# Moving two spectrum loads and a state table behind an FFT reload, and three stores to other DMA queues, in a one-core S4 convolution and MLP gradient kernel

## The chip, the core and the metric

The kernel runs on one core of one Trainium2 chip. The metric is device time in microseconds (us) of one launch. The core has TensorE (PE; its weight loads are listed as PEld), VectorE (DVE), ScalarE (ACT), GpSimd (POOL) and SyncE (SP). SP, ACT and POOL each issue DMA transfers from a queue of their own; an instruction that waits in such a queue holds up all that stand behind it.

## The reference

The forward function mixes two branches by a gate, g = sigmoid(sum of u * gate_w):

```python
dt = exp(log_dt); logdA = dt * (A_re + 1j*A_im); dB = dt * (B_re + 1j*B_im)
P = exp(logdA[:, :, None] * l)                # l = 0..2047
K = einsum("dn,dnl,dn->dl", C, P, dB).real    # 448 x 2048 convolution kernel
a = irfft(rfft(u padded) * rfft(K padded))[:L] + u * Dskip
b = relu(u @ w1 + b1)**2 @ w2 + b2            # 448 -> 1792 -> 448
out = g * a + (1 - g) * b
```

The reference returns this output and the gradients of all parameters and of u for a given grad_out: fifteen outputs. L is 2048, D is 448, N is 256; the inputs and outputs are bf16.

## The kernel before, in words

The FFT convolutions are done as two stages of matmuls with constant matrices. `Ker.fwd1` (lines 224 to 246) is the first stage: for two halves hh and four groups q it multiplies 16 row tiles by `F1`, copies the results from PSUM to a staging buffer, and stores each of the eight staging buffers (448 KB) to a DRAM scratch `gd`. The store goes through DRAM because the second stage needs the data in another layout: `Ker.load_s1` (line 250) loads a quarter of gd back on SP's queue, and it depends on all eight stores. `Ker.fwd2` (line 260) is the second stage. `Ker.inv1` (line 296) and `inv2` (lines 313 and 315) are the inverse transform, which stores to a scratch `hd` (line 300) from a ring of six staging buffers and is loaded back by `load_hs` (line 306).

There are three transforms forward: u, the scaled gradient, and K. The first two run in the first part, and their spectra are stored to `sp_d`. The part in the middle runs the MLP (`dense`), interleaved by hand with the state-space recurrences over 14 chunks of channels (`period`). Until `order` is entered (`tc.manual_schedule()`, near 215 us) the order of instructions on each engine comes from a planner with a cost model; after it, each engine runs in the order in which the program is written.

The first layer of the MLP computes 14 tiles of the hidden activations (`hidden`, lines 663 to 683) and stores each to a scratch `rT_d` (512 KB) when its second half is done. The first two stores go to GpSimd's queue, the later ones to SP's.

The tail begins when K has been built and stored to `k_d`. It loads K back into `xs` (`reload_k`), loads the first spectrum, runs the last chunk's backward pass (`back_z`, line 1162), loads two more spectra by `load_sx` (line 1431, 896 KB each on SP's queue) and the state table of the second parameter tile by `load_st` (line 1422, 512 KB on GpSimd's queue), and then runs `fwd1` on K with `K.lean` set. With `lean`, each staging buffer is stored by one transfer. The eight staging buffers are all different, so fwd1 does not wait for its stores. After it come `back_p` (lines 1173 and 1175), the eight steps of `param_grads` for the first parameter tile (line 1494 and those after it, on DVE and ACT, with outputs stored by GpSimd, line 1497), the last steps of the MLP, the four loads of gd, and the last `back_s`. The three remaining spectra are then loaded.

The loop that follows takes each quarter q of the spectrum of K: `product(w, q)` multiplies it by a loaded spectrum on DVE (lines 1568 and 1569), `fwd2` computes the next quarter, and `back1` runs `inv1` on the product. For w = 0 all four quarters are done, then hd[1] is loaded back; for w = 1 the same is done with hd[2]. The spectra are read in the order (0,0), (0,1), (0,2), (0,3), (1,0), (1,1), (1,2), (1,3). The two loaded before fwd1 are (0,3) and (1,0). The state table of the second parameter tile is read by `param_grads(1)`, between the products of w = 1. Two loops over the quarters then finish the two outputs.

Of the kernel before, what the change touches and what calls it, by code (L numbers as in the profile page):

```python
# [162 lines left out]
class Ker:  # L163
# [62 lines left out]
    def fwd1(self, rhs, gd, stage, act_first=0, between=None):  # L226
        nc = self.nc
        for hh in range(2):
            for q in range(4):
                self.act_only = 4 * hh + q < act_first  # L230
                st = stage[self.stage_i % len(stage)]
                self.stage_i += 1
                for j2 in range(2):
                    ps = self.pair()
                    for jj in range(2):
                        nc.tensor.matmul(ps[jj][:, 0:D], lhsT=self.F1[:, hh * 128:(hh + 1) * 128], rhs=rhs(q * 4 + j2 * 2 + jj), start=True, stop=True)  # L236
                    self.evac2(st[:, 2 * j2:2 * j2 + 2, :], ps)
                dst = bass.AP(tensor=gd, offset=(16 * hh + q * 4) * 128 * D, ap=[[D, 128], [128 * D, 4], [1, D]])
                if self.lean:
                    (self.q2 if q % 2 == 0 or hh == 1 else nc.sync).dma_start(dst, st)  # L240
                else:
                    for g2 in range(2):
                        half = bass.AP(tensor=gd, offset=((16 * hh + q * 4) * 128 + 64 * g2) * D, ap=[[D, 64], [128 * D, 4], [1, D]])
                        (self.q2 if g2 == 0 else nc.sync).dma_start(half, st[64 * g2:64 * g2 + 64])
                if between:
                    between(4 * hh + q)
# [73 lines left out]
def kernel(ctx, tc, A_u, A_A_re, A_A_im, A_B_re, A_B_im, A_C_re, A_C_im, A_log_dt, A_Dskip,  # L320
# [3 lines left out]
    nc = tc.nc  # L324
    V, S, G_, T_ = nc.vector, nc.scalar, nc.gpsimd, nc.tensor
# [5 lines left out]
    def dscr(name, n, dt=bf16):  # L331
        return nc.dram_tensor(name, (n,), dt, kind="Internal")
# [9 lines left out]
    rT_d = dscr("rT_d", F * L)  # L342
# [58 lines left out]
    def carve(n, dt=bf16, k=0):  # L401
        nonlocal o
        w = n * (2 if dt == fp32 else 1)
        if k:
            r = RA[:, 7168:7168 + w]
        else:
            r = RA[:, o:o + w]
            o += w
        return r.bitcast(fp32) if dt == fp32 else r
    for nm, src in (("Ar", A_A_re), ("Ai", A_A_im), ("Br", A_B_re), ("Bi", A_B_im), ("Cr", A_C_re), ("Ci", A_C_im)):  # L410
        r = carve(2 * D).rearrange("p (h d) -> p h d", h=2)
# [16 lines left out]
    SB = K.t("S25", [P, 12800])  # L428
# [216 lines left out]
    def force(i):  # L645
        if held and held[0][0] <= i:
            release()

    def rows_of(tensor, j):
        return bass.AP(tensor=tensor, offset=256 * j, ap=[[8 * HW, P], [HW, 8], [1, 256]])  # L650

    def load_w1(jp):
        b = w1b[jp % 2]
        G_.dma_start(b[:, 0:3], bass.AP(tensor=B_w1.tensor, offset=B_w1.offset + 256 * jp, ap=[[F, P], [P * F, 3], [1, 256]]))
        for h in range(2):
            G_.dma_start(b[64 * h:64 * h + 64, 3], bass.AP(tensor=B_w1.tensor, offset=B_w1.offset + 384 * F + 256 * jp, ap=[[F, 64], [1, 256]]))

    def wide(half, w, x):

        pss = [K.ps(b, [P, 512]) for b in BK["h"]]  # L660
        for k in range(2):
            for dt in range(DT - 1):
                T_.matmul(pss[k][:], lhsT=w[:, dt], rhs=x(2 * half + k)[:, dt], start=(dt == 0), stop=False, skip_group_check=True)  # L663
        for k in range(2):
            h = slice(64 * k, 64 * k + 64)
            T_.matmul(pss[k][:], lhsT=w[h, 3], rhs=x(2 * half + k)[h, 3], start=False, stop=True, tile_position=(64 * k, 0), skip_group_check=True)  # L666
        return pss

    def hidden(j, half):
        pss = wide(half, w1b[j // 2 % 2][:, :, P * (j % 2):P * (j % 2) + P], lambda lb: UT[:, :, 512 * lb:512 * lb + 512])  # L670
        if half == 0:
            rcur[j], prev = rts.pop(0)
            rts.append((rcur[j], j))
            force(prev)
        r = rcur[j]
        for k in range(2):
            lb = 2 * half + k
            S.activation(r[:, 512 * lb:512 * lb + 512], pss[k][:], ACT.Relu, bias=b1_f[:, j:j + 1])  # L678
        if half == 1:
            if hold:  # L680
                held.append((j, lambda: nc.sync.dma_start(rows_of(rT_d, j), r)))
            else:
                (G_ if j < 2 else nc.sync).dma_start(rows_of(rT_d, j), r)
            if j % 2 == 1 and j // 2 + 2 < HP:
                load_w1(j // 2 + 2)

# [36 lines left out]
    def first_layer():  # L723
# [3 lines left out]
        for half in range(2):  # L727
            hidden(0, half)
            yield
# [417 lines left out]
    def back_z(c, yt, j, banks=None):  # L1147

        nonlocal zi
        h = j // 2  # L1150
        if (c, h) not in zbs:
            zbs[c, h] = zr[zi % 2]
            zi += 1
        psF = None if banks else K.psF()
        psz = [K.ps(i, [P, 512]) for i in banks] if banks else [psF[:, t] for t in range(2)]
        for b in range(16):
            for t in range(2):
                T_.matmul(psz[t][:, 32 * b:32 * b + 32], lhsT=yt[64 * t:64 * t + NY, b, :], rhs=DKc[64 * t:64 * t + NY, c % 2, 16 * (j % 2) + b].rearrange("p s a -> p (s a)"),  # L1158
                          start=True, stop=True, tile_position=(64 * t, 0), skip_group_check=True)
        if banks:  # L1160
            for t in range(2):
                S.copy(run(zbs[c, h][:, 0:1], 16 * (j % 2) + 1024 * t, [64, NA], [32, 2], [1, 16]), run(psz[t][:, 0:1], 0, [1, NA], [NA, 2], [32, 16]))
        else:
            S.copy(run(zbs[c, h][:, 0:1], 16 * (j % 2), [1024, 2], [64, NA], [32, 2], [1, 16]), run(psF[:, 0, 0:1], 0, [512, 2], [1, NA], [NA, 2], [32, 16]))  # L1164
# [13 lines left out]
    def back_s(c, Q):  # L1178

        nonlocal sps  # L1180
        cc = c % GC
        if cc == 0:
            sps = K.ps("S", [P, GC, 2, P])
        for r in range(2):
            for t in range(2):
                if r + t > 0:
                    yield
                for a in range(NA):
                    for h in range(2):
                        T_.matmul(sps[64 * h:64 * h + 64, cc, r, :], lhsT=Q[h][r][:, 1024 * t + 64 * a:1024 * t + 64 * a + 64], rhs=(nident if r == 0 and t == 1 else ident)[:],  # L1190
                                  start=(cc == 0 and r == 0 and t == 0 and a == 0), stop=(cc == GC - 1 and r == 1 and t == 1 and a == NA - 1),
                                  tile_position=(0, 64 * h), skip_group_check=True)
        if cc == GC - 1:
            stS = K.t("st", [P, 512], fp32, bufs=2)
            S.copy(stS[:], sps[:].rearrange("p q r n -> p (q r n)"))  # L1195
            for x in range(4):
                G_.dma_start(bass.AP(tensor=s_d, offset=(x * D + 64 * (c // GC)) * 256, ap=[[512, 32], [1, 512]]), stS[32 * x:32 * x + 32])  # L1197
# [221 lines left out]
    def load_st(dt, b, q_):  # L1419
        z = DSZ[dt]  # L1420
        STs[dt] = b[:, 0:2048].bitcast(fp32).rearrange("p (h k r n) -> p k r h n", h=2, k=2, r=2)
        q_.dma_start(b[:z, 0:2048].bitcast(fp32).rearrange("p (x n) -> p x n", x=4), bass.AP(tensor=s_d, offset=dt * P * 256, ap=[[256, z], [D * 256, 4], [1, 256]]))
# [7 lines left out]
    def load_sx(w, q, k, qe=nc.sync):  # L1430
        qe.dma_start(slots[k], bass.AP(tensor=sp_d[w], offset=q * 8 * D, ap=[[16 * 2 * D, P], [1, 8 * D]]))
        return slots[k].rearrange("p (a r d) -> p a r d", a=4, r=2)
# [6 lines left out]
    sx = {(0, q): load_sx(0, q, q - 1) for q in (1, 2)}  # L1439
# [28 lines left out]
    V.tensor_tensor(out=xv[0:1, 0], in0=xv[0:1, 0], in1=dsk_bc[0:1].rearrange("o (c g e) -> o c g e", g=NG, e=16), op=ALU.add)  # L1468
    for j in range(4):
        back_z(NCH - 1, YTs[NCH - 1][j], j, NT[2 * (j % 2):2 * (j % 2) + 2])  # L1470
    for q in (3, 4):
        sx[q // 4, q % 4] = load_sx(q // 4, q % 4, q + 6)
    load_st(1, SB[:, 10752:12800], G_)
    K.pairs = 3

    Gt = Pt[:, 0:7168].rearrange("p (t d) -> p t d", d=D)
# [73 lines left out]
    s1k = [b.rearrange("p (a d) -> p a d", d=D) for b in (Yf[:, 0:3584], Yf[:, 3584:7168], SB[:, 6272:9856], SB[:, 0:3584])]  # L1550
    for q in range(4):
        K.load_s1(gd[2], q, s1k[q])
    sums = back_s(NCH - 1, [Qs.pop((NCH - 1, h)) for h in range(2)])
    sx[1, 3] = load_sx(1, 3, 4)
    sx[1, 1] = load_sx(1, 1, 2)
# [63 lines left out]
    for q in range(4):  # L1619
# [30 lines left out]
        for g in range(NG):  # L1650
            dst = bass.AP(tensor=o0.tensor, offset=o0.offset + (16 * g + 2 * q) * D, ap=[[64 * D, 32], [8 * D, 2], [1, 2 * D]])
            G_.dma_start(dst, ao[32 * g:32 * g + 32].rearrange("p (h x) d -> p h (x d)", h=2))
    close(3)
    for q in range(4):
# [9 lines left out]
        for g in range(NG):  # L1664
            dst = bass.AP(tensor=o1.tensor, offset=o1.offset + (16 * g + 2 * q) * D, ap=[[64 * D, 32], [8 * D, 2], [1, 2 * D]])
# [51 lines left out]
```

## Time and profile before

| what | value |
|---|---|
| median of three runs | 741.79 us (738.06 to 744.74) |
| time of the profiled execution | 742.86 us |
| its span, first to last instruction | 741.1 us |
| granted TensorE clock, mean | 0.912 of full |
| bytes moved by DMA | 176.73 MB, mean 238 GB/s |

Times in the profile are microseconds from the start of the span. A row of the timeline gives the start, the time covered, the engine, the source line, the operation, what it writes and reads by the program's tile names, and how many instructions are merged; in brackets stands how long the engine had been idle and what released it. Engine names that end in q are the engine's queue of DMA instructions or of semaphores. Tile names are those of the storage, so `Y<-gd` is a load of gd into a tile that lies in Y's storage, and `R<-sp` is a load of a spectrum.

### The profile page before, as it was taken

What the parts mean: (1) busy time and instruction counts of PE and PEld (TensorE: products, weight loads), DVE (VectorE), ACT (ScalarE), POOL (GpSimd) and SP (SyncE); (2) the same over time, 40 slices, a digit from 0 to 9 for tenths busy, and PEclk for the clock granted to TensorE, in tenths of its full rate; (3) what the DMA queues carried; (4) which work ended last, traced back from release to release, by engine and by line L of the source; (5) the groups of instructions that cost most, each with busy time, mean ns of one, the idle gap of its engine ahead of it and who ended that gap; (6) DMA issues with size and microseconds to landing.
All of it is one profiled execution on the core that took longest, in us unless ns stands there. A gap on an engine that the chain in (4) does not pass through costs nothing.

```text
span 741.1 us, 20444 instructions
## 1 busy us (share of the span) xinstructions
PE 626.1 (84%) x8556; PEld 338.3 (46%) x8597; DVE 563.0 (76%) x928; ACT 513.8 (69%) x877; POOL 167.9 (23%) x285
## 2 busy tenths in 40 slices
PE   5957968789899987998999996989989888787666
PEld 2411323333346553655656664655655563433211
DVE  1397587676788566889999899698898886959474
ACT  2796967588777666777788777778744536598555
POOL 2252211111134311111211201102100333311543
PEclk9986976889999999999999999999999988999757
DMA  9898576829477899999998988999997949988995
GB/s 205 184 298 275 180 271 224 299 96 349 171 246 262 241 238 220 170 250 229 212 221 217 217 133 245 249 205 269 210 230 209 275 119 364 345 292 303 315 331 167
DMA packets 205276, 176.73 MB, mean 238 GB/s; under 512 B 122814, under 2 KB 185559, under 8 KB 205055
## 3 DMA queue, kind: packets, MB, share of 16 engines
q1 hardware_dynamic: 181999, 116.78, 63.8%
q0 software_dynamic: 14272, 39.68, 17.4%
q10 hardware_dynamic: 8912, 18.96, 7.0%
q8 instruction: 67, 1.10, 0.6%
q14 instruction: 26, 0.21, 0.1%
HBM read 82.90 MB, written 64.32 MB: 199 GB/s over the span
## 4 chain that ended last, share of the span: by engine, by line
PE 46%; DVE 16%; DMA 14%; ACT 11%; issue 11%; POOL 1%; ACTq 0%; DVEq 0%; POOLq 0%; SPq 0%
PE psN L663 7%; PE psS L1190 5%; PE psN L699 5%; PE psN L919 4%; PE psX L1096 3%; DMA R<-Y 3%; DVE Y L1035 3%; DVE Y L1032 3%; DVE F L1033 2%; PE psX L699 2%; PE psN L666 2%; PE psF L1158 2%; PE psN L260 2%; DMA out_dram<-X 2%; PE psN L236 2%
## 5 line engine op out<-in xcount | busy, mean ns | idle before, releaser
L699 PEld LDWEIGHTS <-U 128*128 128x128 bf16 x448 | 40.9, 100 | 44.0 <-issue 14.1
L1164 ACT CAST P<-psF 128x1024 bf16<-128x1024 f32 x52 | 53.1, 1022 | 8.9 <-PE psF L1158 8.7
L1032 DVE TENSOR_TENSOR Y<-Y,F 128x1024 bf16<-128x1024 bf16 (+3 forms) x70 | 47.9, 685 | 2.7
L1035 DVE TENSOR_TENSOR Y<-Y,F 128x1024 bf16<-128x1024 bf16 (+3 forms) x70 | 48.1, 688 | 2.4
L663 PEld LDWEIGHTS <-S 128*128 128x128 bf16 x336 | 29.9, 100 | 43.4 <-issue 17.3
L699 PE MATMUL psN<-S,U 128*128 128x449 bf16 x224 | 48.0, 355 | 1.1 <-issue 1.1
L663 PE MATMUL psN<-S 128*128 128x512 bf16 x153 | 46.2, 414 | 1.9 <-issue 1.0
L1033 DVE TENSOR_TENSOR F<-Y,F 128x1024 bf16<-128x1024 bf16 (+3 forms) x70 | 47.3, 675 | 0.0
L699 PE MATMUL psX<-D,U 128*128 128x448 bf16 x160 | 37.2, 370 | 2.1 <-ACT D L705 2.1
L1197 POOL DMA_DIRECT2D s_d<-st x28 | 14.8, 536 | 103.5 <-ACT st L1195 103.5
L691 ACT ACTIVATE U<-psN 128x1024 bf16<-128x1024 bf16 x35 | 36.1, 1031 | 1.5 <-PE psN L690 1.5
L678 ACT ACTIVATE U<-psN,b_f 128x512 bf16<-128x512 f32 x48 | 31.1, 688 | 6.2 <-PE psN L666 4.3
L1158 PEld LDWEIGHTS <-R 41*128 41x128 bf16 x1792 | 26.8, 93 | 18.3 <-issue 15.9
L919 PEld LDWEIGHTS <-U 128*128 128x128 bf16 x252 | 24.4, 101 | 23.5 <-issue 3.8
L1158 PE MATMUL psF<-S,R 41*128 41x32 bf16 x1664 | 29.5, 174 | 5.3 <-ACT P L1164 5.3
L663 PE MATMUL psN<-K,S 128*128 128x512 bf16 x100 | 26.6, 379 | 5.3 <-issue 2.9
L919 PE MATMUL psN<-S,U 128*128 128x448 bf16 x140 | 29.9, 368 | 0.0
L296 PEld LDWEIGHTS <-cb_MI 64*128 64x128 bf16 x256 | 15.7, 99 | 30.4 <-issue 22.0
L1190 PEld LDWEIGHTS <-M 128*64 128x64 bf16 x896 | 25.8, 110 | 3.8 <-issue 2.6
L1190 PE MATMUL psS<-ident,P 128*64 128x128 bf16 x896 | 27.5, 219 | 0.0
L1190 PEld LDWEIGHTS <-P 128*64 128x64 bf16 x896 | 25.9, 110 | 0.0
L1173 DVE TENSOR_TENSOR M<-P,R 128x2048 bf16<-128x2048 bf16 x14 | 17.1, 1221 | 10.2 <-ACT P L1164 10.2
(417 smaller groups left out, 1684.0 us busy)
## 6 DMA issues: line engine op xcount, KB each, us to landing
sp<-K ACTq DMA_DIRECT2D x8, 896.0 KB, 6.8
rT_d<-U SPq DMA_DIRECT2D x10, 512.0 KB, 5.1
hd<-F SPq DMA_DIRECT2D x11, 448.0 KB, 10.4
X<-gd SPq DMA_DIRECT2D x5, 896.0 KB
U<-dhT_d SPq DMA_DIRECT2D x5, 896.0 KB
rec_d<-F ACTq DMA_DIRECT2D x2, 1920.0 KB, 9.0
hd<-st ACTq DMA_DIRECT2D x8, 448.0 KB
rec<-rec_d POOLq DMA_DIRECT2D x14, 256.0 KB, 5.6
```

What stands on the lines that cost most here:

```text
L663: T_.matmul(pss[k][:], lhsT=w[:, dt], rhs=x(2 * half + k)[:, dt], start=(dt == 0), stop=False, skip_group_check=True)
L678: S.activation(r[:, 512 * lb:512 * lb + 512], pss[k][:], ACT.Relu, bias=b1_f[:, j:j + 1])
L691: S.activation(hn[j % 2][:, 8 * th:8 * th + 8, :], ps[:], f)
L699: T_.matmul(ps[:, 0:w], lhsT=hn[j % 2][:, t, :], rhs=rhs[:, t, :], start=(t == 0), stop=(t == LT - 1))
L919: T_.matmul(ps[:, 0:D], lhsT=src[j][:, P * x:P * x + P], rhs=ws[:, j, :], start=(j == 0), stop=(j == FT - 1))
L1032: V.tensor_tensor(out=run(yb, dst, [64, X2], [d0[1], n // d0[1]], [1, d0[1]]), in0=run(yb, 0, [64, X2], *src), in1=pr, op=ALU.mult)
L1033: V.tensor_tensor(out=run(vb, 0, [n, X2], [d0[1], n // d0[1]], [1, d0[1]]), in0=run(yb, 0, [64, X2], *src), in1=pi, op=ALU.mult)
L1035: return V.tensor_tensor(out=hi, in0=hi, in1=run(vb, n, [2 * n, W2], [-n, 2], [1, n]), op=ALU.add)
L1096: T_.matmul(ps[32 * g:32 * g + 32, i], lhsT=run(xb, 2048 * (1 - t) + w, [W2, 32]), rhs=Y[:, w, t, 0:NY], start=(h == 0 and t == 0), stop=( ...
L1158: T_.matmul(psz[t][:, 32 * b:32 * b + 32], lhsT=yt[64 * t:64 * t + NY, b, :], rhs=DKc[64 * t:64 * t + NY, c % 2, 16 * (j % 2) + b].rearran ...
L1164: S.copy(run(zbs[c, h][:, 0:1], 16 * (j % 2), [1024, 2], [64, NA], [32, 2], [1, 16]), run(psF[:, 0, 0:1], 0, [512, 2], [1, NA], [NA, 2], [ ...
L1190: T_.matmul(sps[64 * h:64 * h + 64, cc, r, :], lhsT=Q[h][r][:, 1024 * t + 64 * a:1024 * t + 64 * a + 64], rhs=(nident if r == 0 and t == 1 ...
```

## The change

Four places change. In `fwd1` with `lean`, which only the tail's call uses, the stores of the second half (hh = 1) alternate between GpSimd's and SP's queue as those of the first half do; before, all four of the second half were on GpSimd's. The loads of the spectra (0,3) and (1,0) and of the state table move from ahead of that `fwd1` to behind the four loads of gd. In `hidden`, the store of the third tile (j = 2) goes to GpSimd's queue instead of SP's; this store is in the first part, not in the tail.

```diff
                 if self.lean:
-                    (self.q2 if q % 2 == 0 or hh == 1 else nc.sync).dma_start(dst, st)
+                    (self.q2 if q % 2 == 0 else nc.sync).dma_start(dst, st)
...
             else:
-                (G_ if j < 2 else nc.sync).dma_start(rows_of(rT_d, j), r)
+                (G_ if j < 3 else nc.sync).dma_start(rows_of(rT_d, j), r)
...
         back_z(NCH - 1, YTs[NCH - 1][j], j, NT[2 * (j % 2):2 * (j % 2) + 2])
-    for q in (3, 4):
-        sx[q // 4, q % 4] = load_sx(q // 4, q % 4, q + 6)
-    load_st(1, SB[:, 10752:12800], G_)
     K.pairs = 3
...
     for q in range(4):
         K.load_s1(gd[2], q, s1k[q])
+    for q in (3, 4):
+        sx[q // 4, q % 4] = load_sx(q // 4, q % 4, q + 6)
+    load_st(1, SB[:, 10752:12800], G_)
     sums = back_s(NCH - 1, [Qs.pop((NCH - 1, h)) for h in range(2)])
     sx[1, 3] = load_sx(1, 3, 4)
```

`self.q2` is GpSimd's queue here (`K.q2 = G_`), `G_` is GpSimd, `nc.sync` is SP.

## The prediction, as put on record

> **What bounds the kernel now.** I read the page first, then the chain of waits from 600 us on, then the tail by stretches and by engine. The page's chain of what ended last says that no engine sets the whole time, PE the most with 46%:
>
> ```profile
> span 741.1 us, 20444 instructions
> PE 46%; DVE 16%; DMA 14%; ACT 11%; issue 11%; POOL 1%; ACTq 0%; DVEq 0%; POOLq 0%; SPq 0%
> ```
>
> The tail edits act between 608 and 690 us. The queue of SyncE and GpSimd's instructions show who sends what there:
>
> ```profile
> 610.39 2.50 SPq L1431 DMA_DIRECT2D R<-sp  x2
> 613.02 0.77 POOL L1422 DMA_DIRECT2D S<-s_d  x1 [4.22 <-PE psN L236]
> 618.81 3.39 SPq L240 DMA_DIRECT2D gd<-X  x2
> 625.87 1.50 POOL L240 DMA_DIRECT2D gd<-Y  x2 [0.31 <-ACT Y L220]
> 626.62 5.89 DMA gd<-Y
> 637.54 0.57 PE L260 MATMUL psN<-Y,P 128*64 128x448 bf16 x4 [4.34 <-DMA Y<-gd]
> ```
>
> The two spectra (R<-sp) and the state table (S<-s_d) leave before the first FFT stage of K writes gd. Of its eight stores, the last is issued at 626.62, lands 5.89 us later, at 632.5, and only then may SP load gd back (Y<-gd); PE has stood for 4.34 us when it gets the first quarter. That looks like the bound, but VectorE says otherwise:
>
> ```profile
> 625.83 1.22 DVE L1173 TENSOR_TENSOR M<-P,R 128x2048 bf16<-128x2048 bf16 x1
> 637.64 0.08 DVE L1528 DVE_READ_ACCUMULATOR Y<-Y,dtc,R 128x1 f32 x1
> 638.15 0.62 DVE L211 CAST Y<-psN 128x448 bf16<-128x448 f32 x1 [0.43 <-PE psN L260]
> ```
>
> From 625.83 to 637.72 it runs without a gap (back_p, then all of param_grads(0)). The evacuation of fwd2's first result stands behind that in its queue and waited for PE only 0.43 us. The late reload therefore costs the path 0.43 us, not 4.34.
>
> The transfers by stretch (columns after the span: busy time of PE, PEld, DVE, ACT, POOL; granted clock, DMA share, GB/s):
>
> ```profile
> 618.00:632.00 14.00, 13.45 (x62) 6.34 (x61) 13.19 (x18) 8.52 (x17) 5.45 (x8) 0.88 0.99 335
> 636.00:652.00 16.00, 14.06 (x208) 8.89 (x209) 12.34 (x13) 10.71 (x21) 6.72 (x13) 0.89 1.01 407
> 652.00:660.00 8.00, 7.11 (x58) 3.25 (x59) 4.05 (x2) 8.00 (x18) 0.97 (x2) 1.00 1.06 324
> 660.00:664.00 4.00, 3.08 (x28) 1.44 (x25) 3.25 (x2) 4.00 (x9) 0.00 (x0) 1.00 0.43 141
> 664.00:670.00 6.00, 5.14 (x38) 2.72 (x39) 5.95 (x4) 3.50 (x7) 0.00 (x0) 0.72 0.90 265
> 670.00:674.00 4.00, 2.69 (x27) 1.35 (x24) 3.93 (x5) 4.00 (x10) 1.14 (x2) 1.00 0.41 139
> ```
>
> The DMA engines are full to 632 and from 636 to 660, then half idle to 674. A second place is bound by transfers:
>
> ```profile
> 670.39 0.38 SPq L300 DMA_DIRECT2D hd<-F  x1
> 673.25 0.34 SPq L306 DMA_DIRECT2D M<-hd  x1
> 676.20 6.24 SPq L300 DMA_DIRECT2D hd<-F  x3
> 688.54 0.53 ACT L210 CAST F<-psN 128x448 bf16<-128x448 f32 x1 [5.38 <-DMA hd<-F]
> ```
>
> SP stores the last piece of hd[1] at 670.39 and may load hd back at 673.25; the stores from 676.20 stand behind those loads, and ScalarE waits 5.38 us for one of them before it can reuse its buffer. So the end follows from when hd[1] has landed, 673.25.
>
> **The change, part by part.** (1) Stores 6 and 8 of the first stage go from GpSimd's queue to SP's.
>
> ```profile
> L240 POOL DMA_DIRECT2D gd<-Y x4: 754/754/754, 623.3 to 626.6; - x4
> L240 SPq DMA_DIRECT2D gd<-X x2: 365/368/370, 618.8 to 621.8; - x2
> gd<-X SPq DMA_DIRECT2D x2, 448.0 KB
> R<-sp SPq DMA_DIRECT2D x4, 896.0 KB
> S<-s_d POOLq DMA_DIRECT2D x1, 512.0 KB, 8.7
> ```
>
> The issue falls from 0.75 to 0.37 us. (2) Two R<-sp and one S<-s_d, 2 x 896 + 512 = 2304 KB or 2.36 MB, no longer stand ahead of the stores. Six stores are left after 622.20 (618.81 + 3.39, where SP's second one is issued): 6 x 448 KB = 2.75 MB, at 335 GB/s 8.2 us, so their data is through at 630.4, and with a tail of 0.6 us (my estimate; the share of the DMA engines ends at about 632, the last store at 626.62 + 5.89 = 632.5) landed at 631.0. The gain is 1.5 us. Its bounds: 0, if the stores and not what was ahead of them fill the engines; and 3.1, if the last, issued at 626.62 as now, lands as quickly as the fastest hd store of the same size did (2.8 us, the least in the line below), at 629.4. I take 1.5, the rate of the row over the same stores.
>
> ```profile
> DMA to landing us min/median/max: 2.8/10.4/13.1
> ```
>
> Of these 1.5 us the path gets 0.43, because VectorE is not free before 637.72. **Term A: -0.43 us**, if the reload is at least that much earlier; 0 if it isn't. If it lets ScalarE and PE run ahead as well, at most the whole 1.5.
>
> (3) The moved loads now run behind the reload. Who needs them:
>
> ```profile
> 660.72 2.02 DVE L1568 TENSOR_TENSOR X<-R,S 128x3584 bf16<-128x3584 bf16 x1 [2.65 <-ACT S L211]
> 670.26 0.72 ACT L1498 ACTIVATE D<-S,dtc 128x512 f32<-128x512 bf16 x1
> ```
>
> The first spectrum is read at 660.72 (the second one product later), the table at 670.26. Behind the reload (4 x 896 KB = 3.67 MB) the first is through after 4.59 MB, at 407 GB/s 11.3 us after about 634.5, near 646, the second near 648: 14 us ahead of need. GpSimd issues the table after its param_grads stores, near 637, which puts load_raw(1) back 0.77 us; it feeds the same step at 670.26. Cost of both nothing, as long as products and inv1 cover them. SP issues them in some 0.4 us each, with nothing due in its queue before the first hd store, near 649.
>
> (4) What is late next is the hd[1] stores, which share SP's ring with the moved loads. From 636 to 670 the rows above move 6.51 + 2.59 + 0.56 + 1.59 = 11.25 MB; with 2.36 more it is 13.6, of which seven hd stores are 3.2 MB. Pure store traffic and pure loads run at
>
> ```profile
> DMA packets 1608, 1.42 MB, mean 355 GB/s; under 512 B 49, under 2 KB 1605, under 8 KB 1607
> ```
>
> (687 to 691, SP's queue alone) and 407 GB/s: 3.2 / 0.355 + 10.4 / 0.407 = 9.0 + 25.6 = 34.6 us. Started 1.5 us earlier, at 634.5, the ring is empty at 669.1, 0.9 us before the last hd store is issued (670.39 - 0.43 = 669.96). **Term B: 0.** Without the head start and with the stores at the mixed 324 GB/s it is empty at 671.5, and the last store lands 1.5 us late; nothing absorbed would be 2.36 MB at 407 GB/s, 5.8 us late. I take 0, since the idle stretches 660 to 664 and 670 to 674 are seen.
>
> At this row a rule of the skill speaks against the change: the Trainium skill, DMA: Bandwidth & Descriptors, section Queues, rings and completion order, says that each DMA engine takes the descriptors of one queue in ring order. The trace agrees, in the 5.38 us that ScalarE waits for a store behind loads. By the rule alone, with no idle time counted, the sum would be +5.4 us.
>
> (5) rT_d's third store (j = 2) goes from SP to GpSimd.
>
> ```profile
> 66.50 16.96 SPq L250 DMA_DIRECT2D X<-gd  x2
> 92.70 0.56 SPq L683 DMA_DIRECT2D rT_d<-U  x1
> 97.33 0.32 SPq L250 DMA_DIRECT2D X<-gd  x1
> 98.10 0.72 POOL L713 DMA_DIRECT2D DBT_d<-S  x1 [11.21 <-ACT S L712]
> L683 POOL DMA_DIRECT2D rT_d<-U x2: 907/930/952, 75.5 to 80.8; - x2
> ```
>
> SP holds it from 83.46 to 92.70, but what follows waits for its buffer until 97.33, so nothing is won. On GpSimd its 0.93 us lie inside an idle time of 11.21. **Term C: 0.** Uncovered it would cost those 0.93 us.
>
> **The sum**: 742.86 us for the profiled execution (741.1 span, 1.8 around it) - 0.43 + 0 + 0 = 742.4. The median of the three runs is 741.79, 1.07 lower, so there **741.4 us**; its own range is 740.3 (all 1.5 us pass) to 742.9 (term A empty, 1.1 lost in term B).
>
> **The rivals.** *Backlog* (slower): the moved loads hold SP's ring beyond 669.96, the last hd[1] store lands late, the load of hd starts after 673.25 and ScalarE's wait at 688.54 moves with it. It decides once the ring empties after 669.96. Price 1.5 - 0.43 = 1.1 to 5.8 - 0.43 = 5.4 us; middle 3.2, so 745.0. For it: no idle time from 636 to 660. Against it: the two half-empty stretches.
>
> *PE stays fast* (faster). Where the first stage starts, PE stands and then runs slowly:
>
> ```profile
> 615.68 0.91 PE L236 MATMUL psN<-F,cb_F1BD 128*128 128x448 bf16 x2 [2.20 <-issue]
> 616.00:622.00 6.00, 6.00 (x19) 2.56 (x18) 4.03 (x6) 3.72 (x7) 1.51 (x2) 0.56 1.02 392
> q8 instruction: 1, 0.02, 5.9%
> ```
>
> If the 2.20 us were due to the full DMA engines (the last line is a code packet moved at 613 to 614, just then) and the clock stayed up, the gain would be 2.2 + 6.0 x (1 - 0.56) = 4.8 us, 737.0. Against it: one earlier spectrum and the M2 constants still load until then. The Trainium skill, TensorE: Matmul & The Clock Gate, section What's actually happening, has the clock halve after an idle window of about 3.4 us; by that rule a shorter stand could keep it, and this rival would hold.
>
> *Another order in the first part*: until `order` is entered, a planner puts the instructions in order:
>
> ```profile
> 0.76 0.40 SPq L389 DMA_DIRECT2D U<-in_A_u_dram  x1
> 1.21 0.31 SPq L383 DMA_DIRECT2D prow<-in_gate_w_dram  x1
> ```
>
> Line 389 stands before line 383. Moving one store can reorder its neighbours. If a load then waits as SP waited, 92.70 - 83.46 = 9.2 us are lost, or by luck won; half of that lost gives 746.4. Against it: no consumer of that store is near.
>
> *The stores do not land earlier*: term A is empty, 741.8, within the forecast's range.
>
> **How the numbers follow.** Forecast (740.3 to 742.9) 0.40, backlog 0.25, PE fast 0.10, another order 0.25. A measurement of this kernel tells about 1%, 7.4 us, from no change; the three runs alone lie 738.06 to 744.74, some 3.3 us to either side, and that spread carries a rival over the line. Slower by over 1%: a third of backlog (0.09) and 0.15 of the 0.25 for order: 0.24. Faster: half of PE fast (0.05) and 0.07 of order: 0.12. Within: 0.64. The range reaches 735 (PE fast, with 2 us of the spread) to 750 (backlog's 5.4 and order's middle, with the spread).
>
> **What would show it.** Right: L240 with four stores on each queue; the first Y<-gd near 631; PE's wait before L260 near 3 us and VectorE's gap before 638.15 gone; the idle share at 660 to 664 filled; M<-hd within 0.5 us of 672.8; ScalarE's wait at 688 as before. Wrong: M<-hd after 674 (backlog), PE's 2.20 us gone (PE fast), a different order before 215 us, or any product L1568 that waits for sp.

## The result, and the profile after

The kernel after takes 750.41 us (median of four runs, 748.11 to 753.99), the kernel before beside it 741.62: a ratio of 1.0109, 95% interval 1.006 to 1.0159, so 4.4 to 11.8 us slower. The forecast was 741.4. The profiled execution of after took 748.11 us with a span of 746.3, 5.2 us more than the 741.1 of before. Ratios compare undisturbed runs only, and since the profiled executions of three kernels (table alone, spectra on GpSimd's queue, one spectrum) were slow ones, only their stretches behind the reload are read.

The queue of SyncE, TensorE, VectorE and ScalarE in the tail of after, from the timeline (start, duration, in brackets the idle time before and what ended it), against the rows of before in the prediction:

```profile
631.43 0.81 SPq L250 DMA_DIRECT2D Y<-gd  x2
636.43 0.57 PE L260 MATMUL psN<-Y,P 128*64 128x448 bf16 x4 [4.29 <-DMA out_dram<-rec]
637.04 0.63 DVE L211 CAST Y<-psN 128x448 bf16<-128x448 f32 x1 [0.36 <-PE psN L260]
659.78 2.03 DVE L1568 TENSOR_TENSOR X<-R,S 128x3584 bf16<-128x3584 bf16 x1 [2.65 <-ACT S L211]
666.29 0.91 ACT L220 CAST st<-psF 128x896 bf16<-128x896 f32 x1 [3.12 <-DMA hd<-st]
669.78 0.45 SPq L300 DMA_DIRECT2D hd<-F  x1
677.30 0.34 SPq L306 DMA_DIRECT2D M<-hd  x1
694.05 0.53 ACT L210 CAST F<-psN 128x448 bf16<-128x448 f32 x1 [11.51 <-DMA hd<-F]
706.10 0.82 SPq L306 DMA_DIRECT2D Y<-hd  x2
```

The same last load in before:

```profile
701.30 1.04 SPq L306 DMA_DIRECT2D Y<-hd  x2
```

The reload starts 1.26 us earlier, and the fourth product, the first that reads a moved spectrum, is still 0.94 us ahead (659.78 against 660.72). The last hd[1] store is issued 0.61 us ahead as well, 669.78 for 670.39. But it lands 7.5 us later instead of 2.9: M<-hd comes at 677.30, 4.05 us behind. From there the lag is kept and grows a little: the load of hd[2] is 4.80 us late, the end 5.2. A wait that before did not have, 3.12 us at 666.29, shows that the first hd[1] stores were late too.

The transfers of after by stretch, columns as in the prediction (DMA share and GB/s last):

```profile
614.00:618.00 4.00, 3.28 (x9) 1.28 (x9) 1.29 (x3) 2.13 (x4) 0.78 (x1) 0.50 0.04 16
652.00:660.00 8.00, 7.31 (x62) 3.33 (x60) 4.28 (x3) 8.00 (x18) 0.09 (x1) 1.00 1.05 274
660.00:664.00 4.00, 2.22 (x22) 1.01 (x19) 3.97 (x3) 3.17 (x7) 0.00 (x0) 1.00 0.97 336
664.00:670.00 6.00, 6.00 (x46) 2.94 (x47) 5.66 (x3) 3.71 (x7) 0.00 (x0) 0.72 1.11 359
670.00:674.00 4.00, 2.44 (x25) 1.13 (x21) 3.90 (x6) 4.00 (x9) 1.14 (x2) 1.00 1.05 302
```

And before, where the same 4 us ahead of the FFT stage were full, and the stretch from the first reload to M<-hd, and from there to the load of hd[2]:

```profile
614.00:618.00 4.00, 2.32 (x7) 0.99 (x7) 0.77 (x2) 1.66 (x4) 0.18 (x1) 0.56 1.02 414
632.69:673.25 40.56, 31.88 (x348) 17.30 (x347) 31.98 (x28) 31.16 (x61) 10.08 (x20) 0.92 0.88 307
673.25:701.30 28.05, 21.68 (x163) 8.48 (x163) 20.48 (x39) 17.86 (x37) 11.44 (x22) 0.88 1.00 346
```

The two stretches in after:

```profile
631.43:677.30 45.87, 36.67 (x388) 19.13 (x387) 36.80 (x33) 35.53 (x71) 12.27 (x23) 0.93 0.97 327
677.30:706.10 28.80, 17.82 (x127) 6.44 (x123) 15.53 (x33) 12.38 (x25) 10.68 (x20) 0.81 0.95 330
```

Read the last two columns. Before moved 40.56 x 0.307 = 12.5 MB from the reload to M<-hd at a share of 0.88, after 45.87 x 0.327 = 15.0 MB at 0.97. The idle stretches on which term B rested are filled, and that was not enough: the engines were busy for 0.88 x 40.56 = 35.7 us before and 0.97 x 45.87 = 44.5 after, so 8.8 us of work came into 4.9 us of idle time. The 4 us at 614 to 618, where before moved 1.7 MB while little else depended on the engines, now stand empty (0.04). The second stretch is 0.75 us longer, which is no more than it varies in the four kernels with the loads in place (28.05 to 29.36 us): it follows M<-hd.

A second, local loss lies in the first part, where the prediction's term C had nothing. The timeline near 215 us, before and then after:

```profile
215.23 0.62 SPq L378 DMA_DIRECT2D M<-c_Ew  x1
216.29 0.79 DVE L1073 COPY Y<-rec 128x256 bf16<-128x256 bf16 x1
217.71 2.57 POOL L1264 MEMSET Y<- 128x2944 bf16 x1
227.45 3.73 PE L1131 MATMUL psN<-ident,Y 128*128 128x128 bf16 x64 [0.66 <-DVE Y L1035]
237.87 1.88 SPq L1229 DMA_DIRECT2D dk_d<-st  x2
```

```profile
214.16 0.62 SPq L378 DMA_DIRECT2D M<-c_Ew  x1
215.02 2.57 POOL L1264 MEMSET Y<- 128x2944 bf16 x1
215.23 2.96 DVE L1073 COPY Y<-rec 128x256 bf16<-128x256 bf16 x1
228.52 3.73 PE L1131 MATMUL psN<-ident,Y 128*128 128x128 bf16 x64 [2.80 <-DVE Y L1035]
238.94 2.35 SPq L1229 DMA_DIRECT2D dk_d<-st  x2
```

From M<-c_Ew to the first dk_d<-st are 22.64 us before and 24.78 after. In after GpSimd's memset starts 0.2 us ahead of VectorE's copy, the copy takes 2.96 us for 0.79, and TensorE waits 2.80 for 0.66. In this pair the loss does not last: U<-sp, ahead of the reload, is issued at 607.64 in after and at 608.03 in before.

### The profile page after: what moved, and what is told of

Its sections match the earlier page's. It is cut to its first block, busy times and chain, and to the rows that moved or that the text cites. A ratio compares the mean times of both kernels' runs of the same rounds, so it can differ in the third digit from the quotient of the medians.

```text
span 746.3 us, 20434 instructions
## 1 busy us (share of the span) xinstructions
PE 622.4 (83%) x8556; PEld 335.9 (45%) x8597; DVE 566.0 (76%) x928; ACT 513.4 (69%) x877; POOL 167.2 (22%) x284
## 4 chain that ended last, share of the span: by engine, by line
PE 40%; DMA 16%; DVE 14%; issue 13%; ACT 12%; POOL 2%; SPq 2%; ACTq 0%; DVEq 0%; POOLq 0%
PE psN L919 6%; PE psS L1190 5%; PE psN L663 5%; PE psN L699 4%; DMA U<-in_A_u_dram 3%; PE psX L1096 3%; DVE Y L1035 2%; DVE Y L1032 2%; DMA hd<-F 2%; DMA R<-Y 2%; DVE F L1033 2%; PE psF L1158 2%; ACT U L691 1%; PE psN L236 1%; PE psN L690 1%
## 5 line engine op out<-in xcount | busy, mean ns | idle before, releaser
L919 PEld LDWEIGHTS <-U 128*128 128x128 bf16 x252 | 24.1, 100 | 22.7 <-issue 2.7
L1173 DVE TENSOR_TENSOR M<-P,R 128x2048 bf16<-128x2048 bf16 x14 | 17.1, 1221 | 10.9 <-ACT P L1164 10.9
```

The lines of the kernel that those rows point to most:

```text
L919: T_.matmul(ps[:, 0:D], lhsT=src[j][:, P * x:P * x + P], rhs=ws[:, j, :], start=(j == 0), stop=(j == FT - 1))
```

## The experiments

The theory was that the moved loads hold the DMA engines past the time when the hd[1] stores want them; the rivals were that the loss comes from the stores' queue, or from the first part. A queue's transfers, in the order in which they were issued, are called its ring here.

**One edit at a time.** The moved loads alone (before, with the loads and the table behind `load_s1`):

```diff
-    for q in (3, 4):
-        sx[q // 4, q % 4] = load_sx(q // 4, q % 4, q + 6)
-    load_st(1, SB[:, 10752:12800], G_)
...
     for q in range(4):
         K.load_s1(gd[2], q, s1k[q])
+    for q in (3, 4):
+        sx[q // 4, q % 4] = load_sx(q // 4, q % 4, q + 6)
+    load_st(1, SB[:, 10752:12800], G_)
```

> The kernel before with one edit of the three: the two spectra and the state table move behind the reload; stores 6 and 8 of the first stage stay on GpSimd's queue. Theory (the moved 2.36 MB holds SP's ring and the DMA engines past the time when the hd[1] stores want them): this edit carries all of the loss. The first of these hd stores (issued near 648) lands after 664, ScalarE waits about 3 us for it near 666, the load M<-hd starts 3.5 to 5 us later than before's 673.25, and the time is 5 to 8 us above before. Rival 1 (the third rT_d store changes the first part): no more than 1 us above before, M<-hd within 0.5 us of 673. Rival 2 (the two stores that share SP's ring with the spectra make the reload and all behind it late): within 1 us of before, M<-hd near 673.

Measured: ratio 1.0095 (1.0061 to 1.0128), some 7 us. The stretch from the first reload to M<-hd:

```profile
632.16:676.49 44.33, 35.44 (x379) 18.85 (x377) 35.26 (x32) 34.50 (x69) 11.31 (x22) 0.92 0.99 337
```

Mostly as the theory expected: M<-hd is 3.24 us behind that of before, a little under the 3.5 to 5 it had named. The stores alone:

```diff
-                    (self.q2 if q % 2 == 0 or hh == 1 else nc.sync).dma_start(dst, st)
+                    (self.q2 if q % 2 == 0 else nc.sync).dma_start(dst, st)
```

> The kernel before with one edit of the three: stores 6 and 8 of the first stage on SP's queue, loads where they were. Theory: within 1 us of before. The two stores now stand behind two spectra loads in SP's ring, so the reload Y<-gd is not earlier than before's 632.69, at most 1 us later, and VectorE, busy to 637.7, covers up to about 4 us of that. Rival 2 (this edit carries the loss): 5 us or more above before, Y<-gd after 636.

Measured: 0.9967 (0.9931 to 1.0002); M<-hd 41.17 us after the first reload. No loss, and no gain that is shown. The third rT_d store alone:

```diff
-                (G_ if j < 2 else nc.sync).dma_start(rows_of(rT_d, j), r)
+                (G_ if j < 3 else nc.sync).dma_start(rows_of(rT_d, j), r)
```

> The kernel before with one edit of the three: the third rT_d store on GpSimd's queue. Theory: within 1 us of before, all of the tail at the same times. Rival 1 (another order in the first part): 4 us or more above before, with U<-sp already issued 3 us or more after before's 608.03.

Measured: 1.0049 (1.0006 to 1.0092), 3.6 us, with M<-hd 41.50 us after the reload. I had expected nothing. Its timeline has the pair of after, and worse transposes:

```profile
218.28 2.57 POOL L1264 MEMSET Y<- 128x2944 bf16 x1
218.48 2.96 DVE L1073 COPY Y<-rec 128x256 bf16<-128x256 bf16 x1
231.77 5.36 PE L1131 MATMUL psN<-ident,Y 128*128 128x128 bf16 x64 [2.80 <-DVE Y L1035]
```

Both tail edits without it, which is after with `j < 2`:

> The kernel after with the third rT_d store back on SP's queue; the two tail edits stay. Theory (the whole loss lies in the tail and comes from the moved loads): the time of after within 2 us, 5 to 10 us above before, M<-hd within 1 us of 677. Rival (the rT_d store costs the 3.6 us by which it stood above before alone): 3 to 4 us below after, the gain lying ahead of 608 us.

Measured: 1.0096 (1.0056 to 1.0136), M<-hd 45.29 us after the reload, and M<-c_Ew to dk_d<-st back at 22.7 us. The tail edits carry most of the loss; from 1.0096 to after's 1.0109 the time does not tell.

**Which order, or how many bytes.** The first half of the grad_out rows later, in after:

```diff
-        if q == 2:
-            load_rows16((nc.sync, G_), Gt, G2, (0,))
...
-    load_rows16((nc.sync, G_), Gt, G2, (1,))
+    load_rows16((nc.sync, G_), Gt, G2)
```

> The kernel after, with the first half of the grad_out rows (four loads of 224 KB, two on GpSimd's ring and two on SP's) moved from the third inverse step behind the loads of hd[1]. Theory in the form 'loads of two rings together fall from 400 to 274 GB/s and hold up the first hd stores at 652 to 664': with 0.92 MB off that stretch the first hd store lands 2 to 3 us earlier, ScalarE's 3.12 us near 666 goes under 1 us, M<-hd comes to 673.5 to 675 (677.30 in after), and the time is 2 to 4 us below after (1 to 3 us above before). Form 'the store waits only for the spectra ahead of it in SP's own ring': M<-hd stays within 1 us of 677.3, since the rows on GpSimd's ring are not in its way and the ones on SP's ring are behind it, and the time is that of after or 1 us more.

Measured: 1.0103 (1.0053 to 1.0153). M<-hd comes at 674.80, 43.54 us after the reload (45.87), but the stretch behind it grows from 28.80 to 31.33 us, and the end is where it was. The edit moved less than I had thought: GpSimd's queue does not wait for hd[1], so its rows still left early, and only SP's half, 0.46 MB, changed places. All hd stores on ScalarE's queue, out of every ring with loads:

```diff
-    K.q3 = nc.sync
+    K.q3 = nc.scalar
```

> The kernel after, with all eight hd[1] and eight hd[2] stores issued on ScalarE's queue in place of SP's, so that none of them stands behind a load in a ring. Theory 'ring order' (a store costs what stands ahead of it in its ring): the first hd store lands within 5 us of its issue (18 us in after), ScalarE's 3.12 us near 666 and 11.51 us near 694 both go under 1.5 us, M<-hd comes at 671 to 674 (677.30 in after), the last stretch starts 5 to 9 us earlier than after, and the time is 5 to 9 us below after, at or a little under before. Theory 'bytes' (between the reload and the load of hd[2] the DMA engines move all bytes at one rate, so the moved 2.36 MB is paid whatever the order): M<-hd may come earlier, but the load of hd[2] stays within 2 us of after's 706.10 against the reload, and the time within 2 us of after.

Measured: 1.0146 (1.0101 to 1.0192), no gain. ScalarE's waits shrink from 3.12 and 11.51 to 0.90 and 2.63 us, but M<-hd comes 45.12 us after the reload at a DMA share of 0.98. The order in SP's ring does not explain the loss. The same stores moved in before, for hd[2] alone:

```diff
+    K.q3 = nc.scalar
     for q in range(4):
         product(1, q)
```

> The kernel before, with the eight hd[2] stores on ScalarE's queue; nothing of the change. Theory 'ring order': these stores no longer stand behind the four loads of hd[1] (3.67 MB) in SP's ring, ScalarE's 5.38 us near 688.5 go under 1.5 us, hd[2] is loaded 3 to 6 us before 701.30, and the time is 3 to 5 us below before. Theory 'bytes': the loads of hd[1] lose what the stores gain, VectorE's wait ahead of the first L1634 grows from 4.38 by some 3 us, and the time is within 1.5 us of before.

Measured: 1.003 (0.999 to 1.0071). ScalarE's 5.38 us are gone, but VectorE, which waited 4.38 us at 692.24 in before, still waits 4.04 us, at 694.02, for the grad_out rows; the load of hd[2] stays 68.39 us behind the reload (68.61 before). That wait was not the bound. The two moved spectra on GpSimd's queue, in after:

```diff
-        sx[q // 4, q % 4] = load_sx(q // 4, q % 4, q + 6)
+        sx[q // 4, q % 4] = load_sx(q // 4, q % 4, q + 6, G_)
```

> The kernel after, with the two moved spectra loads at their new place but on GpSimd's queue, so the same 2.36 MB moves, none of it in SP's ring ahead of the hd[1] stores. Theory 'ring order': the first hd store lands 8 us or more earlier than in after, M<-hd comes at 672 to 674.5, and the time is 3 to 6 us below after. Theory 'bytes': M<-hd stays at 676 to 678 and the time within 1.5 us of after; the fetch of the spectra then only shares the engines with the reload (the first product L1568 up to 2 us later).

Measured: 1.0072 (1.0037 to 1.0107), M<-hd after 43.77 us: between the two theories. The 7 us that begin 20 us after the reload, in this kernel, then in after. Below each stretch stands what SP's queue (q1) and GpSimd's (q0) moved in it (packets, MB, share of the engines), then GpSimd's first issue of grad_out rows (P<-in_grad_out_dram):

```profile
661.65:668.65 7.00, 6.31 (x55) 2.88 (x53) 4.05 (x2) 7.00 (x16) 2.86 (x7) 1.00 1.03 372
q1 hardware_dynamic: 936, 2.06, 80.9%
q0 software_dynamic: 255, 0.52, 20.8%
667.14 0.98 POOL L356 DMA_DIRECT2D P<-in_grad_out_dram  x2 [0.38 <-PE psF L260]
```

```profile
651.43:658.43 7.00, 6.31 (x53) 2.92 (x51) 4.05 (x2) 7.00 (x15) 0.66 (x2) 1.00 1.04 288
q1 hardware_dynamic: 193, 1.25, 66.1%
q0 software_dynamic: 184, 0.76, 37.4%
648.07 0.99 POOL L356 DMA_DIRECT2D P<-in_grad_out_dram  x2
```

In this kernel the rows leave GpSimd's queue only at 667.14, at the end of the stretch, so its 372 GB/s are the rate almost without them; in after they left from 648.07 on and run beside the spectra, at 288. The kernel after without the grad_out rows (the two calls of `load_rows16` go, and the sums that use the rows read older data):

> The kernel after without the eight loads of the grad_out rows (1.84 MB); the sums that use them read older data. It leaves out bytes of the stretch that have nothing to do with the moved loads. Theory 'bytes': 1.84 MB at 389 GB/s are 4.7 us, so the load of hd[2] comes 69 to 71 us after the first reload (after 74.67, before 68.61), ScalarE's 11.51 us near 694 shrink to some 6, and the time comes to within 3 us of before, 3 to 6 us below after. Theory 'ring order': M<-hd keeps its 45.9 us behind the first reload (before 40.6), and the time its distance to before within 2 us.

Measured: 1.0008 (0.9972 to 1.0043). The same 7 us, and the stretch to M<-hd:

```profile
658.81:665.81 7.00, 6.31 (x55) 2.89 (x51) 4.05 (x2) 7.00 (x16) 0.00 (x0) 1.00 1.02 403
638.81:678.19 39.38, 30.19 (x349) 16.80 (x348) 30.57 (x26) 30.99 (x61) 8.75 (x17) 0.96 0.92 341
```

Without rows, SP's spectra and hd[1] stores move at 403 GB/s. Neither theory gave the size: bytes at one rate gave 4.7 us up to the load of hd[2], and 8.5 were gained there (74.67 to 66.20), 6.5 of them up to M<-hd. It is the row loads that make the mixture slow, not two rings at once. In before at 10 to 14 us SP's ring moves row loads of grad_out (32 partitions each) and little else, and in after at 640 to 644 both rings are busy without any:

```profile
10.00:14.00 4.00, 4.00 (x30) 2.12 (x28) 1.38 (x2) 0.00 (x0) 1.12 (x3) 1.00 1.02 212
640.00:644.00 4.00, 4.00 (x108) 3.42 (x106) 3.96 (x3) 3.46 (x6) 0.54 (x1) 0.92 1.03 407
q1 hardware_dynamic: 164, 1.05, 65.9%
q0 software_dynamic: 164, 0.58, 37.4%
```

Two rings together reach 407 GB/s, and the rows, alone in one ring, 212; why they are slower these runs do not show. Six of the eight row loads, 1.38 MB, lie ahead of M<-hd in after: at 212 GB/s that is 6.5 us, the gain up to M<-hd, and the 0.46 MB that changed places in the kernel with the first rows later are 2.2 us (M<-hd came 2.33 us earlier). Both are estimates from the one row of before. In after's 7 us the parts, 1.25 MB at 403 and 0.76 at 212 GB/s, come to 6.7 of the 7.3 us of engine time; the rest is not explained.

**By size.** The table alone moved (0.52 MB), and one spectrum alone (0.92 MB):

```diff
-    load_st(1, SB[:, 10752:12800], G_)
...
+    load_st(1, SB[:, 10752:12800], G_)
```

> The kernel before with only the state table (512 KB) moved behind the reload; spectra and stores as before. Theory 'bytes' (from the reload to the load of hd[2] the DMA engines are the bound, and 2.36 MB cost 6.06 us there, 389 GB/s): 0.52 MB cost 1.3 us, so the load of hd[2] is issued 69.5 to 70.5 us after the first reload (before 68.61, after 74.67), and the time is 0.5 to 2.5 us above before. Theory 'ring order' (only what stands in SP's ring ahead of the hd[1] stores costs): the table is on GpSimd's ring, so 68.6, and no change.

Measured: 0.9971 (0.9931 to 1.001), M<-hd 42.01 us after the reload, the load of hd[2] 71.02. Inconclusive: the times show no loss, and 42.01 is 0.3 above the largest of the kernels with this part unchanged (40.56 to 41.74).

```diff
-    for q in (3, 4):
-        sx[q // 4, q % 4] = load_sx(q // 4, q % 4, q + 6)
+    sx[0, 3] = load_sx(0, 3, 9)
...
+    sx[1, 0] = load_sx(1, 0, 10)
```

> The kernel before with only one of the two spectra (sx[1, 0], 0.92 MB) moved behind the reload. From the first reload to M<-hd the DMA engines were busy 0.88 of 40.56 us before and 0.97 of 45.87 after. Theory 'threshold' (the first 12%, 4.9 us or 1.6 MB at 337 GB/s, are free, and what goes beyond is paid in full): 0.92 MB fit, so M<-hd is issued 41 to 42 us after the first reload, the DMA share rises to 0.92 to 0.95, and the time is within 2 us of before. Theory 'linear' (every moved byte costs the same 4.1 us per 2.36 MB): 42.5 to 43 us, the share stays near 0.9, and the time is 2 to 4 us above before.

Measured: 0.9895 (0.9819 to 0.9971), from two runs of this kernel, too few for a gain to be claimed. The stretch:

```profile
639.08:680.16 41.08, 32.28 (x353) 17.35 (x353) 32.40 (x28) 31.41 (x61) 10.40 (x20) 0.92 0.95 326
```

41.08 us with the share risen from 0.88 to 0.95: in this one execution one spectrum fits into the idle time. Two and the table, 2.36 MB, do not: 44.33, 45.29 and 45.87 us. That speaks for a threshold and against a price per byte, which had named 42.5 to 43.

**Tries to do better.** The raw parameter loads of step 1 ahead, in before and with the stores:

```diff
     load_st(0, R2[:, 13824:15872], G_)
+    load_raw(1, SB[:, 3584:5120], G_)
...
-    load_raw(1, SB[:, 3584:5120], G_)
```

> The kernel before with the six raw parameter loads of step 1 (0.79 MB on GpSimd's queue, issued at 637 to 640.5) moved ahead to 586, behind the raw loads of step 0, where the DMA engines are about half idle from 590 to 606. It is the opposite of the change: bytes leave the bound stretch. Theory 'bytes': the load of hd[2] comes 66 to 67.2 us after the first reload (before 68.61), the time 1 to 3 us below before. Theory 'ring order': these loads were in no ring that a hd store uses, so 68.6, and within 1 us of before.

> The kernel before with two edits: stores 6 and 8 of the first stage on SP's queue (which alone stood at a ratio of 0.9967), and the raw loads of step 1 moved ahead to 586. A try at a kernel faster than both. Theory 'bytes': 2 us from the loads, and 0 to 2.5 us from the stores if that ratio was not spread: 739 to 743 where before is 744, the load of hd[2] 66 to 68.5 us after the first reload. Theory 'ring order': no more than the stores bring, 68.6 or above.

Measured: 1.014 (1.0094 to 1.0186) and 1.0124 (1.0076 to 1.0171). The loads went over a part of S that is still in use (the second output is computed from other data), and U<-sp came at 622.92 and 621.60 for 608.03: the loss lies ahead of the tail. As tests of the bytes they fail; M<-hd, at 41.80 and 41.54 us, did not come earlier either. The grad_out rows together, ahead of M<-hd:

```diff
-            load_rows16((nc.sync, G_), Gt, G2, (0,))
+            load_rows16((nc.sync, G_), Gt, G2)
...
-    load_rows16((nc.sync, G_), Gt, G2, (1,))
```

> The kernel before with the second half of the grad_out rows issued with the first, ahead of the hd[1] loads: two loads (0.46 MB) leave SP's ring behind M<-hd, where the DMA engines are full (1.00 of the 28.05 us to the load of hd[2]), for the half idle time ahead of it. Theory 'threshold': M<-hd still 40.5 to 42 us after the first reload, the stretch from M<-hd to the load of hd[2] 1 to 1.5 us shorter than 28.05 to 29.2, the time 0.5 to 2 us below before. Theory 'linear': M<-hd later by 0.8 us or more, and no gain in the sum of both stretches (68.6 to 70.4).

> The kernel before with two edits: stores 6 and 8 of the first stage on SP's queue (0.9967 alone), and both halves of the grad_out rows issued together. A try at a kernel faster than both. Threshold: 1 to 4 us below before, from the rows 1 us and from the stores what of their 2.5 us was not spread. Linear: what the stores bring alone, 0 to 2.5 us.

Measured: 1.0018 (0.9977 to 1.0059) and 0.9985 (0.9943 to 1.0028). Not as the threshold had it: M<-hd came 44.13 and 43.09 us after the reload, in the first at a mean share of 0.87. SP's queue shows four row loads ahead of the last two hd[1] stores:

```profile
666.76 2.23 SPq L356 DMA_DIRECT2D P<-in_grad_out_dram  x4
669.46 0.38 SPq L300 DMA_DIRECT2D hd<-st  x1
671.14 0.77 SPq L300 DMA_DIRECT2D hd<-F  x1
678.02 0.34 SPq L306 DMA_DIRECT2D M<-hd  x1
```

The mean hides when the engines were busy: a share of 0.37 from 660.89 to 665.89, then 0.97 and 0.95 to 673.89, while the rows moved. So bytes that come right ahead of the last stores count although there was idle time before; whether by their place in the ring or by the engines' time, this run does not tell. The opposite, all rows on GpSimd's queue (and the same with the two stores on SP's):

```diff
-            load_rows16((nc.sync, G_), Gt, G2, (0,))
+            load_rows16((G_,), Gt, G2, (0,))
...
-    load_rows16((nc.sync, G_), Gt, G2, (1,))
+    load_rows16((G_,), Gt, G2, (1,))
```

> The kernel before with all eight loads of the grad_out rows on GpSimd's queue (it issues nothing from 653 to 672), none in SP's ring. Theory 'place in the ring' (in the kernel with the rows ahead, two more of these loads on SP's queue in front of the last two hd[1] stores brought M<-hd 3 us later at a DMA share of 0.69, so what stands directly ahead of the last stores counts even where the engines are not full): M<-hd is issued 39 to 40.5 us after the first reload (40.6 to 41.5 in the three kernels with that part unchanged), the stretch from M<-hd to the load of hd[2] is 27 to 28.5 us, and the time 1 to 3 us below before. Theory 'engine time alone': the same bytes move in the same stretch, so 41 to 42 us, and within 1 us of before.

> The same with stores 6 and 8 of the first stage on SP's queue as well; a try at a kernel faster than both. Place in the ring: 2 to 4 us below before. Engine time alone: within 2 us of before.

Measured: 0.9983 (0.9944 to 1.0022) and 0.9976 (0.9939 to 1.0013). M<-hd comes after 39.95 and 41.49 us, and the stretch behind it is 26.49 and 26.50 us for 28.05 to 29.36. The 39.95 is what the place in the ring had named (39 to 40.5), the 41.49 what engine time had (41 to 42), so this does not tell them apart; some 2 us are gained behind M<-hd, and a kernel faster than before is not shown.

**The memset.** The rT_d edit alone, with the memset moved:

```diff
-    G_.memset(Y[:, :, :, NY:64], 0.0)
...
     load_y(1, G_)
+    G_.memset(Y[:, :, :, NY:64], 0.0)
```

> The kernel with the rT_d edit alone, and GpSimd's memset of the zero columns of Y (L1264, 2.57 us) written three steps later, behind the load of the next records. In the six kernels with the rT_d edit this memset starts 0.2 us before VectorE's copy of the seeds (L1073), the copy takes 2.96 us and TensorE waits 2.80 us ahead of L1131; in the kernels without it the memset starts 1.4 us after the copy, the copy takes 0.79 and the wait is 0.67. Theory 'the memset holds the copy': with the memset later the copy takes 0.8 us again, the wait ahead of L1131 is under 1 us, the issue of dk_d<-st comes 22.5 to 22.9 us behind that of M<-c_Ew (24.8 to 26.4 in the six), and the time is that of before within 2 us. Theory 'the third store itself is what is late' (the store's data or its place on GpSimd's queue delays the stage): the copy may be short, but the distance stays at 24.8 or more, and the time 3 to 4 us above before.

The timeline of it:

```profile
212.32 0.62 SPq L378 DMA_DIRECT2D M<-c_Ew  x1
213.38 0.73 DVE L1073 COPY Y<-rec 128x256 bf16<-128x256 bf16 x1
216.53 2.57 POOL L1271 MEMSET Y<- 128x2944 bf16 x1
224.54 3.73 PE L1131 MATMUL psN<-ident,Y 128*128 128x128 bf16 x64 [0.67 <-DVE Y L1035]
234.96 2.04 SPq L1229 DMA_DIRECT2D dk_d<-st  x2
```

The copy is back at 0.73, the wait at 0.67, the distance at 22.64. The local loss is the overlap. That it makes up the time is not shown: the ratio, 1.0041 (1.0002 to 1.008), is 3 us above before where 2 at most were expected, and not clearly below the 1.0049 of the kernel with the memset at its place.

## Why the prediction was wrong, point by point

- **Term A** (-0.43) was right in sign in the profiled pair: from U<-sp to the first reload 24.66 us became 23.79, and the whole chain ran about 1 us ahead to 660. Three other kernels that equal after up to there took 25.36 to 25.85 us, so the gain may be spread. VectorE's gap was not closed (0.36 for 0.43) nor PE's wait (4.29 for 4.34, where I had said 3): VectorE's own block started 1.05 us earlier (its first L1173 at 624.78 for 625.83) and the evacuation behind it 1.11 us, so the cover moved along.
- **Term B** (0) is the step that failed. By the prediction's own rows the engines stood idle for 5.2 us from 660 to 674 (4 x 0.57 + 6 x 0.10 + 4 x 0.59), less than the 5.8 us that 2.36 MB take at 407 GB/s, so "half idle" was too generous. The 13.6 MB were divided by 407 and 355 GB/s, the rates of pure loads and pure stores, and SP's ring came out empty at 669.1. Full engines moved the mixture at 327 to 337 GB/s: 634.5 + 13.6 / 0.33 = 675.7, near the measured 677.30. The row to use was quoted: 652 to 660, share 1.06, 324 GB/s, full and yet slow. In after the row loads ran beside spectra there (274 GB/s). The rows are part of the wrong rate: their 1.38 MB stood in the sum at 407 GB/s, 3.4 us, and take 6.5 at the 212 of the row loads alone.
- **Backlog**, the rival, is what happened in the tail, in its upper half: M<-hd was 4.05 us late in the profiled pair and, counted from the reload, 4.1 in the means of three kernels with the loads moved (45.16) and three without (41.08); ScalarE's wait moved with it, 11.51 us. The rule that was weighed there, ring order by the Trainium skill, DMA: Bandwidth & Descriptors, section Queues, rings and completion order, gave +5.4; its sum was near, but with the stores in a ring of their own M<-hd was as late (45.12). The full engines carried this loss. That the ring decides where they are not full is not shown, since in the kernel with 44.13 us they were full around the last stores.
- **Term C** (0) failed too. The store itself is hidden, as argued; the 0.93 us on GpSimd's queue cost nothing there. What I left out is that GpSimd's later work changes its time against VectorE's: in the six kernels with this edit and the memset at its place the copy took 2.96 us, in the thirteen without it at most 0.80.
- **Another order in the first part** had the right place and the wrong mechanism: VectorE, ScalarE and TensorE keep their order; GpSimd loses a wait of 1.51 us ahead of its L654 load, and so the memset moves. What that wait was, the trace does not name. The stage lost 2.1 to 3.8 us, as the transposes ran at full clock or not.
- **PE stays fast** did not occur: TensorE still stood 1.90 us there, and the clock at 614 to 618 is 0.50 (0.56 before), with the DMA engines idle. In this execution that slow start is not the transfers' doing.
- The sum by the runs: some 4 us in the tail and 2 to 4 in the first part, less up to 0.9 ahead of the reload, against 4.4 to 11.8 measured. The parts do not add up everywhere: in the profiled pair the tail alone makes the 5.2 us, and the two kernels with the loads moved and no rT_d edit stand some 7 us above before, 3 more than the stretch to M<-hd holds. The last stretch, from the load of hd[2] to the end, is 40.20 to 41.76 us in the three kernels with the moved loads and 38.45 to 39.80 in the three without, but 40.98 and 41.98 in two others without them (the rows on GpSimd's queue, the hd[2] stores on ScalarE's); whether it belongs to the loss stays open.

## What to carry to other kernels

Before moving a load to a later place, add up the bytes and the busy share of the stretch it goes to and of the stretch it leaves: a load that runs in DMA time that nobody waits for is free there, and the same load behind a dependent store chain is paid as soon as the idle share is used up. Take the rate from a stretch with the same kinds of loads and stores at a full share, not from the fastest one. And when a GpSimd instruction is added or taken away, look at what its later non-DMA work will then run beside on VectorE.

## What the runs showed of the hardware that was not expected

- Full DMA engines (share 1.02 to 1.04) moved 212 GB/s with 32-partition row loads in one ring (before, 10 to 14 us), 288 with these beside spectra (after, 651 to 658), 403 with spectra and hd[1] stores (the kernel without rows), and 407 with two rings and no rows (after, 640 to 644). A share of 1 is no rate.
- VectorE's copy of 128x256 bf16 takes 2.96 us when a GpSimd memset of 2.57 us starts 0.2 us ahead of it, and ends 0.60 us after it. The Trainium skill, SBUF — State Buffer, section SBUF: two separate sides, has the two engines share a port pair that one holds for a whole instruction while the other stops. The trace agrees; also in that with the late memset (216.53) VectorE's operations on two inputs under it keep their 0.43 and 1.23 us, which that section allows for a GpSimd operation that does not read.
- The same wait of TensorE, 2.80 us, left the 64 transposes behind it at 3.73 us in two kernels and at 5.02 to 5.36 in four; in the kernel with the rT_d edit alone the granted clock there was 0.57 at 232 to 236. The Trainium skill, TensorE: Matmul & The Clock Gate, section What's actually happening, puts the fall at about 3.4 us of idling; here a wait of 2.80 us that the profile shows came out both ways.
